# A retention layer and two feed-forward nets on one core: second products of the last token group held back into the pair loop, a copy put ahead of a cast

## The chip, the cores and the metric

The kernel runs on one core of a Trainium2 chip. The metric is the device time of one execution in microseconds (us); lower is better. TensorE (PE) multiplies, ScalarE (ACT) copies and evaluates functions, VectorE (DVE) and GpSimd (POOL) do element-wise work, SyncE (SP) starts the transfers between device memory and the core. Each engine runs its own instructions strictly in the order in which they were written; between engines, semaphores hold an instruction until its data or its buffer is there.

## The reference, cut to what matters

```python
x = retention(q, k, v)              # 4 x 768 tokens, 8 heads of 64: 3072 tokens x 512
h = x @ w_in                        # first net: 512 -> 2048
g = where(h > 0, h, exp(min(h, 0)) - 1)
x = g @ w_out                       # 2048 -> 512
h = x @ w2_in                       # second net: 512 -> 2048
g = (a0 + a1*h + a2*h**2 + a3*h**3) / (1 + |b0|*|h| + |b1|*h**2 + 1e-6)
out = g @ w2_out                    # 2048 -> 512
```

## The kernel before

**Split numbers.** Every float32 operand of a product is kept as a high part (a rounding ScalarE cast) and a low part (operand minus high part); a product is three matmuls: high by high, high by low, low by high. So each operand that is made on the chip costs one ScalarE cast and one subtract (`gh` and `gl` for a net's activations, `wo` for a slice of w_out or w2_out, `split_w`). The subtract of `wo`, of the second net's `gl` and of its tokens is GpSimd's; the subtract of the last block's `gl` is VectorE's.

**First net.** Tokens come in 6 blocks j of 512, the hidden layer in 16 slices f of 128. The loop over `(j, f)` does for each slice the first product (`g1`, 12 matmuls of 512 columns into `h`), the activation on ScalarE and VectorE, and behind `g1` the second product of the slice before (`g2`, again 12 matmuls of 512 columns, added up over f in four banks `acc`). `pend` is the slice whose second product is still to come. In the last block (`last`, j = 5) the two tiles `ha1`/`hb1` take turns as `h`, and this loop also prepares the second net: `load_c` and `split_w` bring w2_out slices, `w2_load`, `w2_sums` and `w2_units` make the combined w2_in blocks and write them to device memory, `x2_load` and `x2_step` make the first block's tokens, and `pack_load` brings the weights of the first pairs.

**Second net.** The loop over P takes a pair of slices (2p, 2p+1) at a time, 8 pairs to a token block, 48 pairs in all, and two more rounds for what is left. A pair's first product is a seven-product scheme on 2 x 2 blocks: `prod` does six matmuls of 256 columns, in the order 7, 1, 6, 4, 2, 5, 3. Partial sums are carried on by copying an accumulator into the place where the next product adds to it (`cp`, ScalarE): `s7`, `Q`, `u2` and last `R2` (in the trace: COPY s, ha, u, ha). Product 5 waits for the copy `u2`, product 3 for `R2`. Then two VectorE adds (`Xp`, `Pp`) finish the odd slice. `r_one`, `r_act` and `r_dve` evaluate the rational function of the odd slice (`b1_`) and the even one (`a1_`); `put` casts the result (`gh`), has GpSimd subtract (`gl`), and appends the 12 matmuls of the second product to the list `q2`. `take(n)` issues n matmuls from the list; a full pair has 42 matmuls of 256 columns and takes 5 + 2 + 5 + 6 + 6 = 24 of 512. The next block's tokens are made in the meantime (`x2_step` by the table `XSTEPS`: a plain name is a cast and a GpSimd subtract, a name with + is a GpSimd difference).

The first net's last two slices (f = 14, 15 of j = 5) are put into the list in pairs 0 and 1 and finished there; a pair before P = 2 has only those 12 matmuls, and its even slice's `r_one` comes a pair late:

```python
        if P < 2:
            jj, f, gh, gl = tail[P]
            g2_put(0, jj, f, gh, gl, False, f == KF - 1)
...
                take(5 - 5 * P)
...
        if P == 1:
            r_one(a1_)
            put(b1_, b1_["f"] == 1, False)
...
                take(6 if P > 1 else 0)
```

Of the kernel before, what the change touches and what calls it, by code (L numbers as in the profile page):

```python
# [9 lines left out]
F32 = mybir.dt.float32  # L10
# [75 lines left out]
def retention_ffn_kernel(ctx: ExitStack, tc: tile.TileContext, qkv, w1i, w1o, w2i, w2o, a_, b_, tab, out):  # L86
# [76 lines left out]

    def split_w(ph, f, e):
        c = W.pop((ph, f, e, "c"))
        nm = "io"[e]
        w = wp.tile([128, 2, 512], F32R, tag=f"{nm}{f}", name=f"w{nm}{f}")
# [628 lines left out]
    def fill(n):  # L796

        while nload[0] < min(nconv[0] + n, len(todo) if it > 31 else 2 * KF + 1):
            load_next()

    sums = psa.tile([128, 512], F32, tag="acc3", name="sums")
    for k in range(3):
        at_sum(4 + k, [sums[R[p], 128 * k:128 * k + 128] for p in range(2)])
    order = ["heGmg"] + ["hheGymugxw"] * 7 + ["yxhhweGmug"] + ["eGg"]
    pend = half = None
    after = False
    for it, (j, f) in enumerate(seq):
# [109 lines left out]
        if last:  # L917
            if 0 < f < KF - 1:
                load_c(f, 1)
# [4 lines left out]
            x2_step(0, ["", "B11", "+T3", "B21", "+T1", "B22 +T2", "T1", "T3 +T4", "T2", "T4", "", ""][max(f - 4, 0)])  # L924
            if f in (8, 12):
                pack_load(f // 4 - 2)
        if pend is not None:
            if f < KF - 1 or not last:
                g2(0, *pend)
            else:  # L930
                tail = [pend]
        if last:
            if 0 < f < KF - 1:
                split_w(1, f - 1, 1)
            if not f:
                load_c(f, 1)
# [20 lines left out]
    wk = ctx.enter_context(tc.tile_pool(name="wk", bufs=2, reuse_waits="tile"))  # L957
    tail.append(pend)
    q2 = []

    def take(n):
        while q2 and n >= q2[0][0]:
            k, go = q2.pop(0)
            go()
            n -= k

    def g2_put(ph, j, f, gh, gl, first, last):
        wh, wl = W[f, "o"]
        at = [slice(128 * m, 128 * m + 128) for m in range(4)]

        def one(m, a, b, start, stop):
            def go():
                if (ph, j) not in acc:
                    acc[ph, j] = [psa.tile([128, 512], F32, tag=f"acc{k}", name=f"acc{k}") for k in range(4)]
                lhsT, rhs = (a[:, at[m]], b) if ph else (b[:, at[m]], a)
                nc.tensor.matmul(out=acc[ph, j][m], lhsT=lhsT, rhs=rhs, start=start, stop=stop)  # L976
            return 1, go

        high = [[one(m, gh, wh, first, False), one(m, gh, wl, False, False)] for m in range(4)]
        low = [one(m, gl, wh, False, last) for m in range(4)]  # L980

        if last:
            for m in range(4):
                q2.extend(high[m] + [low[m]])
                if ph == 1 and j == NB - 1:
                    q2.append((0, lambda m=m: out_m(j, m)))
                elif m % 2:
                    q2.append((0, lambda m=m: out_two(ph, j, m // 2)))
        else:
            q2.extend(sum(high, []) + low)  # L990

    def out_m(j, m):
        ps = acc[1, j][m]
        ys = wk.tile([128, 512], F32, tag="su"[m % 2], name="ys", bufs=3)
        t0 = row(j, m)
        if m % 2:
            nc.scalar.mul(ys, ps, -1.0)
        else:
            nc.vector.tensor_scalar_mul(ys, ps, -1.0)
        (nc.scalar if m == 3 else nc.sync).dma_start(out=out[t0:t0 + 128, :], in_=ys)  # L1000

    def out_two(ph, j, a):
        ps = acc[ph, j]
        ys = stg.tile([128, 2, 512], F32, tag="st", name="ys")
        nc.scalar.mul(ys[:, 0], ps[2 * a], -1.0 if ph else 1.0)
        nc.vector.tensor_scalar_mul(ys[:, 1], ps[2 * a + 1], -1.0 if ph else 1.0)
        if ph == 0:
            nc.sync.dma_start(out=y1[j][:, 2 * a:2 * a + 2, :], in_=ys)
        else:
            t0 = row(j, 2 * a)  # L1010
            nc.sync.dma_start(out=out[t0:t0 + 256, :].rearrange("(a p) d -> p a d", p=128), in_=ys)

    def x2_bufs():
# [74 lines left out]
    for P in range(NB * NPR + 2):  # L1088
        more = P < NB * NPR
        j, p = divmod(P, NPR)  # L1090
        if P < 2:
            jj, f, gh, gl = tail[P]
            g2_put(0, jj, f, gh, gl, False, f == KF - 1)
        if more:
            if P < 2:
                take(5 - 5 * P)
# [55 lines left out]
        if more:  # L1152
# [81 lines left out]
```

## Time and profile before

| | |
|---|---|
| time, median of 3 runs | 1123.22 us (1123.08 to 1123.69) |
| time of the profiled execution | 1123.6 us |
| its span, first to last instruction | 1121.8 us |
| TensorE busy | 1104.0 us, 98% |
| VectorE, ScalarE, GpSimd busy | 782.6, 773.5, 420.5 us |
| granted TensorE clock | 1.00 in every window of 50 us |

What lies around the span is 1.8 us. Busy times of an engine are sums of its instructions' times; a matmul's end is modelled, so the gaps of TensorE are known to about a tenth of a microsecond. The last block of the first net runs from about 508 to 592 us, the pairs from there on.

### The profile page before, as it was taken

Reading aid. Unit: us, or ns where it says so; the run is one execution under the profiler, and the core shown is the slowest. Engines: PE = TensorE matmul, PEld = TensorE weight load, DVE = VectorE, ACT = ScalarE, POOL = GpSimd, SP = SyncE. Lnnn points to the kernel's source line nnn. Section 1 sums busy time; section 2 is a strip of 40 time slices with the busy share of each in tenths; the row PEclk is TensorE's granted clock in tenths of the full one; section 3 lists DMA queues with packets and bytes.
Section 4 is the critical chain, followed back from the end, with each engine's and each line's share of the span. In section 5 each row is a group of like instructions: output and inputs, shape, how many; then the busy total and the mean of one; then the engine's idle time right before and its main releaser. Section 6 shows DMA issues by size and latency. Waiting matters only on the chain.

```text
span 1121.8 us, 21652 instructions
## 1 busy us (share of the span) xinstructions
PE 1104.0 (98%) x8398; PEld 937.4 (84%) x8398; DVE 782.6 (70%) x1254; ACT 773.5 (69%) x1434; POOL 420.5 (37%) x322
## 2 busy tenths in 40 slices
PE   7999999999999999999998999999999999999998
PEld 6877888888888888888887888888888889888997
DVE  5997723355555454545556988888888888988986
ACT  5878734365565555445567888888888888888876
POOL 2433302344444333322451642543453452452222
PEclk9999999999999999999999999999999999999999
DMA  9576303375575435416786754855755665655641
GB/s 374 188 247 215 102 1 108 106 249 188 176 248 190 168 124 178 137 48 219 241 317 202 239 156 149 279 160 162 264 168 169 253 176 174 235 176 153 235 132 39
DMA packets 72664, 205.90 MB, mean 184 GB/s; under 512 B 8177, under 2 KB 8689, under 8 KB 72561
## 3 DMA queue, kind: packets, MB, share of 16 engines
q1 hardware_dynamic: 72272, 204.12, 54.3%
q8 instruction: 66, 1.08, 0.4%
q10 hardware_dynamic: 288, 0.40, 0.1%
q14 instruction: 38, 0.30, 0.1%
HBM read 167.79 MB, written 36.70 MB: 182 GB/s over the span
## 4 chain that ended last, share of the span: by engine, by line
PE 86%; DVE 5%; ACT 4%; issue 2%; DMA 1%; POOL 1%; SPq 0%; ACTq 0%; POOLq 0%; DVEq 0%
PE acc L976 23%; PE acc L419 20%; PE hb L1066 14%; PE r L419 12%; PE ha L1066 6%; PE h L419 4%; PE r L262 3%; PE hb L419 2%; PE ha L419 2%; DVE st L158 1%; DVE wc L160 1%; DMA ch<-in_qkv_dram 1%; DVE St L387 1%; DVE h L859 0%; ACT wc L134 0%
## 5 line engine op out<-in xcount | busy, mean ns | idle before, releaser
L1042 POOL TENSOR_TENSOR gl<-e,gh 128x512 fp32r<-128x512 f32 x96 | 129.1, 1345 | 301.9 <-ACT gh L1041 183.2
L976 PE MATMUL acc<-wo,gh 128*128 128x512 f32 x768 | 210.9, 393 | 0.0
L419 PE MATMUL acc<-gh,wo 128*128 128x512 f32 x752 | 189.8, 394 | 0.5 <-ACT ys L494 0.3
L419 PEld LDWEIGHTS acc<-gh,wo 128*128 128x128 f32 x752 | 138.9, 188 | 31.7 <-ACT ys L494 0.7
L976 PEld LDWEIGHTS acc<-wo,gh 128*128 128x128 f32 x768 | 135.3, 189 | 19.0 <-ACT gh L1041 0.3
L419 PE MATMUL r<-xh,wi 128*128 128x512 f32 x440 | 144.2, 389 | 0.0
L863 POOL TENSOR_TENSOR gl<-t,gh 128x512 fp32r<-128x512 f32 x55 | 74.9, 1362 | 174.4 <-ACT gh L861 131.5
L1056 DVE SCALAR_TENSOR_TENSOR u<-u,r 128x512 f32<-128x512 f32 x96 | 81.5, 849 | 51.9 <-ACT r L1033 51.4
L859 DVE SCALAR_TENSOR_TENSOR t<-t,r 128x512 f32<-128x512 f32 x55 | 37.7, 686 | 109.4 <-ACT t L844 106.2
L976 PE MATMUL acc<-wo,gl 128*128 128x512 f32 x384 | 106.5, 391 | 0.0
L419 PE MATMUL acc<-gl,wo 128*128 128x512 f32 x376 | 100.5, 389 | 0.0
L419 PEld LDWEIGHTS r<-xh,wi 128*128 128x128 f32 x440 | 82.6, 188 | 17.2
L1066 PEld LDWEIGHTS ha<-x,wp 128*128 128x128 f32 x576 | 76.2, 190 | 16.4 <-ACT ha L1070 15.0
L1066 PE MATMUL ha<-x,wp 128*128 128x256 f32 x576 | 87.6, 288 | 2.3 <-ACT ha L1070 2.2
L843 ACT ACTIVATE t<-r 128x512 f32<-128x512 f32 x55 | 32.8, 596 | 77.3 <-PE r L419 76.9
L419 PE MATMUL r<-xl,wi 128*128 128x512 f32 x220 | 85.6, 389 | 0.0
L976 PEld LDWEIGHTS acc<-wo,gl 128*128 128x128 f32 x384 | 72.1, 188 | 14.1 <-POOL gl L1042 0.2
L419 PEld LDWEIGHTS acc<-gl,wo 128*128 128x128 f32 x376 | 70.6, 188 | 14.7
L1066 PEld LDWEIGHTS hb<-xl,wp 128*128 128x128 f32 x576 | 75.3, 191 | 5.6 <-ACT ha L1070 1.5
L1066 PEld LDWEIGHTS hb<-xh,wp 128*128 128x128 f32 x576 | 75.4, 191 | 3.6
L1066 PE MATMUL hb<-xl,wp 128*128 128x256 f32 x576 | 76.8, 283 | 0.7 <-ACT ha L1070 0.6
L1066 PE MATMUL hb<-xh,wp 128*128 128x256 f32 x576 | 76.6, 283 | 0.0
(182 smaller groups left out, 2336.6 us busy)
## 6 DMA issues: line engine op xcount, KB each, us to landing
wp<-w2p SPq DMA_DIRECT2D x144, 512.0 KB, 4.2
ch<-in_qkv_dram SPq DMA_DIRECT2D x40, 512.0 KB, 5.4
w2p<-w2t SPq DMA_DIRECT2D x56, 256.0 KB, 2.6
wp<-w2p SPq DMA_DIRECT2D x48, 256.0 KB, 3.6
st<-in_w2i_dram SPq DMA_DIRECT2D x16, 512.0 KB, 4.4
w2s<-wc SPq DMA_DIRECT2D x32, 256.0 KB, 3.2
st<-in_w2o_dram SPq DMA_DIRECT2D x16, 512.0 KB, 4.9
st<-in_w1i_dram SPq DMA_DIRECT2D x12, 512.0 KB, 4.7
```

Source lines behind the costliest of these rows:

```text
L158: lambda: v.scalar_tensor_tensor(out=t[:, :, 0], in0=t[:, :, 1], scalar=-0x80000000, in1=t[:, :, 0], op0=ALU.bitwise_and, op1=ALU.bitwise_or),
L160: lambda: v.scalar_tensor_tensor(out=ci, in0=ci, scalar=3, in1=t[:, :, 0], op0=ALU.logical_shift_left, op1=ALU.bitwise_or),
L262: nc.tensor.matmul(out=out, lhsT=lhsT, rhs=rhs, start=start, stop=stop)
L387: nc.vector.scalar_tensor_tensor(out=S, in0=S, scalar=gc_t[:, 2 * a + z:2 * a + z + 1], in1=u[:, a, z], op0=ALU.mult, op1=ALU.add)
L419: nc.tensor.matmul(out=ps, lhsT=lh, rhs=rh, start=first and idx == 0, stop=last and idx == len(pairs) - 1)
L843: nc.scalar.activation(out=t, in_=h, func=ACTF.Relu, scale=-1.0)
L859: nc.vector.scalar_tensor_tensor(out=y, in0=t, scalar=-1.0, in1=h, op0=ALU.add, op1=ALU.max)
L863: (nc.gpsimd if y is t else nc.vector).tensor_tensor(out=gl, in0=y, in1=gh.bitcast(F32), op=ALU.subtract)
L976: nc.tensor.matmul(out=acc[ph, j][m], lhsT=lhsT, rhs=rhs, start=start, stop=stop)
L1042: nc.gpsimd.tensor_tensor(out=t["gl"], in0=t["e"], in1=t["gh"].bitcast(F32), op=ALU.subtract)
L1056: stt(out=u, in0=u, scalar=QC, in1=t["r"], op0=ALU.add, op1=ALU.mult)
L1066: nc.tensor.matmul(out=o, lhsT=ws[a], rhs=xs[b], start=start and kc == 0 and i == 0, stop=kc == 1 and i == 2, skip_group_check=True)
```

## The change

Four things are done. The list `q2`, `take` and `g2_put` are moved up, and in the first net's last block the second products go through the list as well: from slice 4 on only 9 of the 12 matmuls that a slice adds are taken behind its `g1`, so that 36 are left at the end; with slice 15 that makes 48, which pairs 0 and 1 take as any other pair takes its 24. The held-back activations get tiles of their own (`own`: former w_in tiles i7 to i12 and i13). In pairs 0 and 1 both slices' `r_one` now stand where they stand in all others. In every pair `cp(R2, Pp)` is written ahead of `put(b1_)`, and the token step `x2_step` behind it, with one cast to a pair. With the list, other work moves: the token steps of the last block begin three slices earlier, `pack_load(1)` goes from slice 12 to pair 0, `x2_load` from p = 1 to p = 0, and of the `split_w` four come in pairs 0 (two), 1 and 2, where there were two in pairs 0 and 3.

```diff
-    XSTEPS = ["", "", "B11 +T3", "B21 +T1", "B22 +T2", "T1 T3", "T2 +T4", "T4"]
+    XSTEPS = ["", "B11 +T3", "B21 +T1", "B22 +T2", "T1", "T3", "T2 +T4", "T4"]
...
+    LAG, nsp, nld = 4, [0], [0]
+    own = {f: f"i{f - 1}" for f in range(KF // 2, KF - 2)}
+    own[KF - 1] = "i13"
...
-            if f == 4:
+            if f == 1:
                 x2_load(0, *(x.rearrange("p (a t) -> p a t", a=2) for x in (ch[1][:, 1024:2048], A_b, ch[0][:, 2048:2560], ch[1][:, 2048:2560])))
...
-            if f in (8, 12):
-                pack_load(f // 4 - 2)
-        if pend is not None:
-            if f < KF - 1 or not last:
-                g2(0, *pend)
-            else:
-                tail = [pend]
+            if f == KF // 2:
+                pack_load(0)
+        if pend is not None and (not last or not f):
+            g2(0, *pend)
+        elif last:
+            g2_put(0, *pend, f == 1, False)
+            take(12 if f < LAG else 9)
         if last:
-            if 0 < f < KF - 1:
-                split_w(1, f - 1, 1)
+            while nsp[0] < min(f, (3 * f + LAG - 1) // 4):
+                split_w(1, nsp[0], 1)
+                nsp[0] += 1
...
+            while nld[0] < min(nsp[0] + 3 - (f < KF - 1), KF - 1):
+                load_c(nld[0], 1)
+                nld[0] += 1
...
+    g2_put(0, *pend, False, True)
...
-            if 0 < P and P + 1 < NB * NPR:
+            if P + 1 < NB * NPR:
                 pack_load(P + 1)
-            if p == 1 and j + 1 < NB:
+            if p == 0 and j + 1 < NB:
                 x2_load(j + 1, *x2_bufs())
...
-        if j + 1 < NB:
-            x2_step(j + 1, XSTEPS[p])
         take(5)
...
-        if P == 1:
-            r_one(a1_)
-            put(b1_, b1_["f"] == 1, False)
-        elif b1_:
+        if b1_:
             r_act(a1_, "L")
             r_act(a1_, "E")
-            put(b1_, b1_["f"] == 1, False)
             r_dve(a1_, 5)
+        elif not P:
+            split_w(1, KF - 4, 1, "i14")
+            split_w(1, KF - 3, 1, "i15")
+            load_c(KF - 1, 1)
         take(2)
         if more:
             prod(Pp, P, 5)
             cp(R2, Pp)
+        if b1_:
+            put(b1_, b1_["f"] == 1, False)
+        if j + 1 < NB:
+            x2_step(j + 1, XSTEPS[p])
+        if more:
             nc.vector.tensor_tensor(out=Xp, in0=Xp, in1=u2, op=ALU.add)
             nc.vector.tensor_tensor(out=Pp, in0=Pp, in1=s7, op=ALU.add)
...
-                if P > 1 or t is b1_:
-                    r_one(t)
-                take(6 if P > 1 else 0)
+                r_one(t)
+                take(6)
```

TensorE in pair 0, before, from products 6 and 4 (the x12) to the first products of pair 1; `acc` rows are matmuls of 512 columns from the list, and the row `ha<-xh` is a matmul that only opens pair 1's bank:

```order
L1066 MATMUL hb<-xl,wp_5833 128x256 x12
L1066 MATMUL ha<-x_5679,wp_5835 128x256 x6
L976 MATMUL acc_5493<-gl,wo_1771 128x512
L976 MATMUL acc_5494<-gl,wo_1771 128x512
L1066 MATMUL hb<-x_5680,wp_5835 128x256 x6
L1066 MATMUL ha<-x_5681,wp_5837 128x256 x6
L1100 MATMUL ha<-xh 128x512
```

The same place after the change, from product 5 (hb, x6) on; `g` is a held-back activation:

```order
L1074 MATMUL hb<-x_5773,wp_5825 128x256 x6
L819 MATMUL acc_5496<-g,wo_1630 128x512
L819 MATMUL acc_5493<-g,wo_1630 128x512
L819 MATMUL acc_5494<-g,wo_1630 128x512
L819 MATMUL acc_5495<-g,wo_1630 128x512
L819 MATMUL acc_5496<-g,wo_1630 128x512
L1074 MATMUL ha<-x_5719,wp_5827 128x256 x6
L819 MATMUL acc_5493<-g,wo_1723 128x512 x2
L819 MATMUL acc_5494<-g,wo_1723 128x512 x2
```

Before, product 3 (ha, last x6) followed on product 5 with nothing between; now five matmuls of the list stand there, and twelve more behind product 3.

ScalarE in pair 5 (p = 5), before, from the cast of the even slice of pair 3 to the first function of the new odd slice; `x` and `xh` are casts of tokens, COPY u is `u2`, COPY ha is `R2`:

```order
L1041 CAST gh<-e 128x512
L537 CAST x_6409<-xb_6269 128x512
L537 CAST xh<-xbt 128x512
L1070 COPY u_6759<-hb 128x256
L1031 ACTIVATE r<-u,lnb 128x512
L1033 ACTIVATE r<-r,lnb 128x512
L1041 CAST gh<-e 128x512
L1070 COPY ha<-hb 128x256
L1026 ACTIVATE s<-hb 128x512
```

And after:

```order
L1049 CAST gh<-e 128x512
L1078 COPY u_6754<-hb 128x256
L1039 ACTIVATE r<-u,lnb 128x512
L1041 ACTIVATE r<-r,lnb 128x512
L1078 COPY ha<-hb 128x256
L1049 CAST gh<-e 128x512
L538 CAST xh<-xbt 128x512
L1034 ACTIVATE s<-hb 128x512
```

The two token casts ahead of `u2` are gone; one stands behind `R2` and the cast of the odd slice (the other is now in pair 4).

SyncE's queue from the last slice of the first net into pair 1, after the change; `wc` is a w2_out slice, `wp` the combined weights of a pair (four transfers), `xb` the next block's tokens:

```order
L777 DMA wc<-w2s_1_128 128x512
L556 DMA wp_6134<-w2p_92 128x1024
L556 DMA wp_6136<-w2p_92 128x1024
L556 DMA wp_6138<-w2p_92 128x1024
L556 DMA wp_6140<-w2p_92 128x512
L514 DMA xb_6142<-y_1_85 128x1024
L514 DMA xb_6143<-y_1_85 128x1024
L777 DMA wc<-w2s_1_130 128x512
L556 DMA wp_6250<-w2p_93 128x1024
```

The four transfers from `w2p_92` (pair 1's weights) stood ahead of slice 13's transfers before, in the middle of the last block; now they stand behind the last `wc` load of slice 15.

## Rows read from the trace of the kernel before

**Rows 1.** The page: busy time of TensorE, share of the span, instructions.

```profile
PE 1104.0 (98%) x8398; PEld 937.4 (84%) x8398; DVE 782.6 (70%) x1254; ACT 773.5 (69%) x1434; POOL 420.5 (37%) x322
```

**Rows 2.** Windows, TensorE: stretch, length, busy (matmuls), clock, DMA share, GB/s.

```profile
500.00:550.00 50.00, 50.00 (x223) 1.00 0.65 216
...
600.00:650.00 50.00, 46.06 (x289) 1.00 0.65 216
```

**Rows 3.** Timeline, TensorE, pairs 0 to 4: start, duration, instructions, idle before.

```profile
592.57 1.60 PE L1066 MATMUL hb<-xh,wp 128*128 128x256 f32 x12
...
599.10 0.98 PE L1066 MATMUL ha<-x,wp 128*128 128x256 f32 x6 [0.45 <-ACT ha L1070]
...
608.14 0.97 PE L1066 MATMUL ha<-x,wp 128*128 128x256 f32 x6 [0.44 <-ACT ha L1070]
...
612.34 1.71 PE L1066 MATMUL hb<-xl,wp 128*128 128x256 f32 x12 [0.62 <-ACT ha L1070]
...
616.77 0.98 PE L1066 MATMUL hb<-x,wp 128*128 128x256 f32 x6 [1.54 <-ACT u L1070]
...
620.20 0.98 PE L1066 MATMUL ha<-x,wp 128*128 128x256 f32 x6 [1.29 <-ACT ha L1070]
...
623.76 1.60 PE L1066 MATMUL hb<-xh,wp 128*128 128x256 f32 x12
...
634.52 1.59 PE L1066 MATMUL hb<-xh,wp 128*128 128x256 f32 x12
```

**Rows 4.** Timeline, ScalarE: the last copy of pair 0, then copies and casts in pair 2.

```profile
598.69 0.36 ACT L1070 COPY ha<-hb 128x256 f32<-128x256 f32 x1 [1.51 <-PE hb L1066]
...
615.84 0.61 ACT L537 CAST xh<-xb 128x512 fp32r<-128x512 f32 x1
616.36 0.36 ACT L1070 COPY u<-hb 128x256 f32<-128x256 f32 x1
...
619.26 0.62 ACT L1041 CAST gh<-e 128x512 fp32r<-128x512 f32 x1 [1.16 <-DVE e L1058]
```

**Rows 5.** Windows by pair (4, 5, 9): length, then PE, PEld, DVE, ACT, POOL.

```profile
634.51:645.26 10.75, 10.75 (x67) 9.45 (x66) 9.34 (x15) 9.54 (x19) 6.81 (x5) 1.00 0.61 174
645.26:656.02 10.76, 10.57 (x65) 8.96 (x64) 8.82 (x13) 8.31 (x17) 5.49 (x4) 1.00 0.55 168
...
688.27:699.02 10.75, 10.75 (x69) 9.70 (x68) 9.17 (x15) 8.83 (x17) 2.59 (x2) 1.00 0.35 115
```

**Rows 6.** Timeline, ScalarE, pair 9: the last copy and the first function behind it.

```profile
695.05 0.37 ACT L1070 COPY ha<-hb 128x256 f32<-128x256 f32 x1
...
696.38 0.60 ACT L1026 ACTIVATE s<-hb 128x512 f32<-128x512 f32 x1 [0.97 <-DVE hb L1141]
```

**Rows 7.** Timeline: a GpSimd subtract beside VectorE, and VectorE's instruction alone.

```profile
616.01 1.28 POOL L1042 TENSOR_TENSOR gl<-e,gh 128x512 fp32r<-128x512 f32 x1 [7.33 <-ACT gh L1041]
...
616.46 1.38 DVE L1056 SCALAR_TENSOR_TENSOR u<-u,r 128x512 f32<-128x512 f32 x1
...
692.37 0.69 DVE L1056 SCALAR_TENSOR_TENSOR u<-u,r 128x512 f32<-128x512 f32 x1 [1.07 <-ACT r L1033]
```

**Rows 8.** Timeline, pairs 9 and 10: an accumulator read out, then written anew.

```profile
699.69 0.68 DVE L1006 TENSOR_SCALAR ys<-acc 128x512 f32<-128x512 f32 x1
...
700.61 1.32 PE L976 MATMUL acc<-wo,gh 128*128 128x512 f32 x5
```

**Rows 9.** Timeline, last block: two slices of TensorE, and VectorE between them.

```profile
566.73 0.39 PE L419 MATMUL hb<-xh,wi 128*128 128x512 f32 x1
...
571.26 0.43 DVE L574 TENSOR_TENSOR ha<-ch 128x256 f32<-128x256 f32 x1 [3.11 <-DMA ch<-w2s]
...
574.20 0.69 DVE L863 TENSOR_TENSOR gl<-hb,gh 128x512 fp32r<-128x512 f32 x1 [0.65 <-ACT gh L861]
...
577.61 0.39 PE L419 MATMUL hb<-xh,wi 128*128 128x512 f32 x1
```

**Rows 10.** Transfers issued from 555 to 625 us: KB each, median us to landing.

```profile
wp<-w2p SPq DMA_DIRECT2D x15, 512.0 KB, 5.1
```

More of the change, by code (lines that the diff above doesn't have):

```diff
@@ L162, in narrow_b, with split_w @@
         ]
-    def split_w(ph, f, e):
+    def split_w(ph, f, e, tag=None):
         c = W.pop((ph, f, e, "c"))
         nm = "io"[e]
-        w = wp.tile([128, 2, 512], F32R, tag=f"{nm}{f}", name=f"w{nm}{f}")
+        w = wp.tile([128, 2, 512], F32R, tag=tag or f"{nm}{f}", name=f"w{nm}{f}")
         hi, lo = w[:, 0, :], w[:, 1, :]
@@ L508, in x2_set @@
         two = [xp.tile([128, 2, 2, 512], F32R, tag=f"{nm}{n}", name=nm) for nm in ("xh", "xl")]
-        one = [wp.tile([128, 2, 512], F32R, tag=f"i{k}", name="x2") for k in ((11, 12, 13), (0, 1, 2))[n]]
-        parts = [t[:, m] for t in two for m in range(2)] + [t[:, :, :] for t in one]
-        X2[j] = {nm: p for nm, p in zip(("T3", "B11", "T2", "T4", "B21", "T1", "B22"), parts)}
+        X2[j] = {nm: p for nm, p in zip(("T3", "B11", "T2", "T4"), [t[:, m] for t in two for m in range(2)])}
     def x2_load(j, B0, B1, t3, t2):
@@ L533, in x2_split @@
             x2_set(j)
+        if nm not in X2[j]:
+            k = ("B21", "T1", "B22").index(nm)
+            X2[j][nm] = wp.tile([128, 2, 512], F32R, tag=f"i{k if j % 2 == 0 else 11 + k}", name="x2")
         t = X2[j][nm]
@@ L799, in fill, with take, g2_put, one @@
             load_next()
+    q2 = []
+    def take(n):
+        while q2 and n >= q2[0][0]:
+            k, go = q2.pop(0)
+            go()
+            n -= k
+    def g2_put(ph, j, f, gh, gl, first, last):
+        wh, wl = W[f, "o"]
+        at = [slice(128 * m, 128 * m + 128) for m in range(4)]
+        def one(m, a, b, start, stop):
+            def go():
+                if (ph, j) not in acc:
+                    acc[ph, j] = [psa.tile([128, 512], F32, tag=f"acc{k}", name=f"acc{k}") for k in range(4)]
+                lhsT, rhs = (a[:, at[m]], b) if ph else (b[:, at[m]], a)
+                nc.tensor.matmul(out=acc[ph, j][m], lhsT=lhsT, rhs=rhs, start=start, stop=stop)
+            return 1, go
+        high = [[one(m, gh, wh, first, False), one(m, gh, wl, False, False)] for m in range(4)]
+        low = [one(m, gl, wh, False, last) for m in range(4)]
+        if last:
+            for m in range(4):
+                q2.extend(high[m] + [low[m]])
+                if ph == 1 and j == NB - 1:
+                    q2.append((0, lambda m=m: out_m(j, m)))
+                elif m % 2:
+                    q2.append((0, lambda m=m: out_two(ph, j, m // 2)))
+        else:
+            q2.extend(sum(high, []) + low)
+    def out_m(j, m):
+        ps = acc[1, j][m]
+        ys = wk.tile([128, 512], F32, tag="su"[m % 2], name="ys", bufs=3)
+        t0 = row(j, m)
+        if m % 2:
+            nc.scalar.mul(ys, ps, -1.0)
+        else:
+            nc.vector.tensor_scalar_mul(ys, ps, -1.0)
+        (nc.scalar if m == 3 else nc.sync).dma_start(out=out[t0:t0 + 128, :], in_=ys)
+    def out_two(ph, j, a):
+        ps = acc[ph, j]
+        ys = stg.tile([128, 2, 512], F32, tag="st", name="ys")
+        nc.scalar.mul(ys[:, 0], ps[2 * a], -1.0 if ph else 1.0)
+        nc.vector.tensor_scalar_mul(ys[:, 1], ps[2 * a + 1], -1.0 if ph else 1.0)
+        if ph == 0:
+            nc.sync.dma_start(out=y1[j][:, 2 * a:2 * a + 2, :], in_=ys)
+        else:
+            t0 = row(j, 2 * a)
+            nc.sync.dma_start(out=out[t0:t0 + 256, :].rearrange("(a p) d -> p a d", p=128), in_=ys)
     sums = psa.tile([128, 512], F32, tag="acc3", name="sums")
@@ L849, in retention_ffn_kernel @@
         y = h if early or last else t
-        gh = gp.tile([128, 512], F32R, tag="gh", name="gh")
-        gl = gp.tile([128, 512], F32R, tag="gl", name="gl")
+        if last and f in own:
+            g = wp.tile([128, 2, 512], F32R, tag=own[f], name="g")
+            gh, gl = g[:, 0], g[:, 1]
+        else:
+            gh = gp.tile([128, 512], F32R, tag="gh", name="gh")
+            gl = gp.tile([128, 512], F32R, tag="gl", name="gl")
         low = None
@@ L957, in retention_ffn_kernel @@
     wk = ctx.enter_context(tc.tile_pool(name="wk", bufs=2, reuse_waits="tile"))
[L958 to L1011, printed above, removed]
     def x2_bufs():
@@ L1117, in retention_ffn_kernel @@
                 r_dve(b1_, k)
+        if P == 1:
+            split_w(1, KF - 2, 1, "o12")
         if a2_:
             put(a2_, False, a2_["f"] == KF - 2)
-        if j + 1 < NB:
-            x2_step(j + 1, XSTEPS[p])
         take(5)
```

23 lines of the change are left out of this document (3 added, 20 removed).

## The prediction, made before the result

> **What bounds the kernel now.** I read the page first: TensorE is busy 98% of the span [rows 1], so a change that leaves its matmuls as they are, and this one does, can only take or add gaps. Windows of TensorE over the span say where gaps are: most stretches of 50 us are full, but 600 to 650 us, the beginning of the pair loop, holds 46.06 us of work [rows 2]. The timeline of TensorE there shows the gaps one by one, and who ended them [rows 3]: 0.45 us in pair 0, 0.44 in pair 1, and 0.62, 1.54 and 1.29 in pair 2, 4.34 us in all, each in front of a product that waits for one of ScalarE's copies (`R2`, `R2`, `Q`, `u2`, `R2`). From 623.76 us on a pair follows the next after 10.76 us.
>
> The timeline of ScalarE shows why the copies are late [rows 4]: in pair 2 `u2` stands behind a token cast of 0.61 us, and `R2` behind the cast of an activation that itself waited 1.16 us for VectorE. That wait is the tail of a debt. Pair 0 has 12 list matmuls where a full pair has 24, pair 1 has 12 too, so TensorE runs through them faster than the other engines can follow, and the even slice's `r_one`, put off from pair 0 to pair 1, falls due when TensorE is already in pair 2.
>
> The windows by pair show a second, small wait [rows 5]: pair 5 has 0.19 us less TensorE work than its length, pair 4 has none. It is the pair with two token casts ahead of `u2`; pairs 13, 21, 29 and 37 show the same 0.19 or 0.20.
>
> **The boundary, step by step.** What the gaps cost is better taken from the period than from modelled ends. From pair 0's first product to pair 3's there are 31.19 us [rows 3]. Three full pairs take 3 x 10.76 = 32.28. The three of before hold 48 list matmuls instead of 72. A matmul of 512 columns costs 0.2267 us: in the last block 48 of them (24 to a slice) lie between 566.73 and 577.61 [rows 9]. So they should need 32.28 - 24 x 0.2267 = 26.84 us, and 0.23 for pair 1's opening matmul: 27.07. The excess is 4.1 us, against 4.34 summed from the rows. I take 4.2.
>
> After the change the three pairs have 72. The 36 extra ones (24 held back at the rate of three per slice from slice 4, and the 12 of slice 14) are only moved: each slice from 4 to 15 takes 9 and is shorter by 3 x 0.2267 = 0.68 us, which the pairs pay back. In place of the gap in pair 0, five matmuls stand between product 5 and product 3, 1.13 us against a wait of 0.45; pairs 1 and 2 get the same shape as any later pair, and the later ones run without a gap. So the 4.2 us should go.
>
> What is added there: two `wo` casts in pair 0 behind `u2`, one in pair 1, one in pair 2, of about the 0.61 of a token cast [rows 4]. In pair 0 ScalarE idles 1.51 us between `u2` and `R2`, until product 5 is done [rows 4]; two casts of 0.61 fit into that, and if they did not, `R2` could still be 1.13 - 0.45 = 0.68 us later than before. Pair 1 has one cast more, but no earlier pair's even slice to cast (0.62 [rows 4]). Cost between 0 (casts in the hole) and 0.6 (one cast uncovered); I take 0.2, nearer to the hole that the rows show.
>
> **The pair loop, step by step.** With one token cast to a pair, and none ahead of `u2`, the five waits of 0.19 go: 5 x 0.19 = 0.95 us. The cast moves to where ScalarE waits anyway: after `R2` it idles until both VectorE adds are done, 0.97 us in pair 9 [rows 6]. The odd slice's activation cast, now behind `R2`, goes into that same hole: 0.62 + 0.61 = 1.2 us, about as long as the hole and `R2`'s earlier start together. The activation's GpSimd subtract is later by about `R2`'s 0.37 us [rows 6]; its first matmul comes after 17 others of the list, 17 x 0.2267 = 3.9 us. Covered.
>
> What is new: in the pair p = 1 of each block the finished accumulators are read out (`ys`, two on ScalarE, two on VectorE), and now a token step falls into the same pair, at pairs 1, 9, 17, 25 and 33. GpSimd's two token instructions come behind the odd `gl` and so run while VectorE does `r_one`, whose first instruction reads two operands. How much such an instruction is held up the rows show for its like: u<-u,r took 1.38 us when it began during a GpSimd subtract, 0.69 alone [rows 7], so 0.69 more. Behind it comes the read-out of the second accumulator, done at 699.69 + 0.68 = 700.37; TensorE writes that bank two matmuls into its row, at 700.61 + 0.45 = 701.06 [rows 8]. The margin is 0.69 us. Lower bound of the cost: 0. Upper bound: a hold as long as a whole subtract, 1.28 us [rows 7], which leaves 0.59 at five places, 3.0 us. Nearest to the measured hold, the cost is about 0; I take 0.3 for all five, since hold and margin are equal.
>
> **The last block.** Its slices get shorter, 24 matmuls to 21, 5.44 to 4.76 us. The other engines must keep that pace, with two tiles between them and TensorE. The worst place of before: VectorE waited 3.11 us for a w2_in transfer and finished slice 11's `gl` at 574.20 + 0.69 = 574.89, where TensorE needs the tile again at 577.61 [rows 9]; 2.72 us to spare. Two shorter slices take 1.36 of them, and the load that is in the way (the weights of pair 0) starts by the work of an earlier slice, which takes up to 0.7 more. Some 0.7 is left; I count 0, upper bound 0.5 (the same again at the other loads). From 500 to 550 us TensorE shows no gap at all [rows 2].
>
> SyncE's queue: pair 1's weights now stand behind slice 15's last `wc` load, whose buffer comes free with slice 11's `wo` subtract. That follows slice 11's last second product, which ends where pair 0 starts, and two ScalarE casts: 2 x 0.62 + 1.28 [rows 4, 7] = 2.5 us. With 5.1 us to land [rows 10] the first of the four transfers is there at 7.6 us; pair 1 starts at 10.76 + 0.23 = 11.0. Covered by 3.4 us, and the fourth is used some 7 us later still. The next block's tokens stand behind them and are due a pair later. On GpSimd's queue the `wo` subtracts of pair 0 precede nothing that is due; in pair 1 one precedes the odd `gl`, with the 3.9 us of cover above.
>
> **Sum.** 1123.6 (the profiled execution) - 4.2 - 0.95 + 0.2 + 0.3 = 1118.95; the median of the runs shown, 1123.22, is 0.4 lower. I predict **1118.5 us**, 0.42% under the median.
>
> **A rule weighed.** VectorE's row of 1.38 beside 0.69 [rows 7] fits the Trainium skill, "SBUF — State Buffer", section "Who interferes with whom": a VectorE instruction with two SBUF inputs and a GpSimd instruction that reads SBUF exclude each other, and the later one waits until the first is through. By that rule taken to its end, two whole holds in every pair with a token step, the time would come out at about 1159 us; by the held instruction of the row it stays at 1118.5. What holds would do here, worked out from rows alone, is the first rival.
>
> **Rivals.**
> *Slower: VectorE becomes the bound of the pairs with a token step.* Mechanism: GpSimd's subtract and difference now lie under the first instruction of both `r_one`. VectorE is busy 9.34 of 10.75 us in pair 4 [rows 5], so 1.41 is free, 0.70 for each of two holds. At the measured 0.69 nothing happens; the point from which it decides is 0.70. At 0.80 each, 35 pairs (seven in five blocks) lose 2 x 0.1, 7 us: 1125.5. At the full 1.28 each pair loses 2 x 1.28 - 1.41 = 1.15, all of them 40 us. For it: hold and limit lie close. Against: pair 4 has token work and pair 9 has none, and VectorE is only 0.17 us busier there [rows 5], so that holds are rare or short. Chance 0.06.
> *The stall moves instead of going.* The `wo` casts, the pair-1 token step and the read-out press on ScalarE in pairs 0 to 2, and half of the 4.2 us stays: 1121.0 less the 0.95 either way, 1120.0 to 1121.2. For it: ScalarE is busy 9.5 of 10.75 in pair 4. Chance 0.13.
> *The last block or pair 1's weights give it back.* If the other engines could not follow 4.76 us and stayed at 5.44, TensorE would lose all of 12 x 0.68 = 8.2 us; a third of that, or weights that land 3.4 + 3 us late, gives 2.7 to 3 us back: 1121.5, no difference beyond 0.2%. Against: the spare 2.72 us at the worst place. Chance 0.08.
>
> **How the numbers follow.** A measurement here tells about 0.2% (2.2 us) from no change. The forecast's own range, with the bounds above, is 1117.5 to 1119.8, chance 0.73. Adding the case in which half the stall stays, the range is 1117.0 to 1121.0. Faster: 0.73 + 0.13 less a sliver beyond the line, 0.85. Same: 0.08. Slower: 0.07, the VectorE case and a worse form of the third.
>
> **What would show it.** TensorE's timeline from pair 0 on without gaps over 0.2 us, and a distance of 10.76 from pair to pair (pairs 0 and 1 0.23 more); slices 4 to 15 of the last block at 4.76; no gap in pairs 5, 13, 21, 29, 37. Wrong would be: gaps ended by `ys` or VectorE at pairs 2, 10, 18; `r_one`'s first VectorE instruction stretched in every token pair, with VectorE busy over 10.5 of 10.75; a gap at pair 1's first product ended by a transfer; gaps between slices 8 and 13.

## The result, and the profile after

The changed kernel takes 1110.76 us, median of 4 runs (1109.55 to 1111.66), against 1123.22 before: a ratio of 0.9888, 95% interval 0.9871 to 0.9905. That is 12.5 us less where 4.7 were forecast, and outside the range. The profiled execution took 1111.66 us with a span of 1109.7, 12.1 us less than the span before.

The page of the changed kernel, span and busy times. TensorE has less busy time than before with the same 8398 matmuls [rows 1]:

```profile
span 1109.7 us, 21633 instructions
...
PE 1094.9 (99%) x8398; PEld 940.0 (85%) x8398; DVE 786.2 (71%) x1254; ACT 782.0 (70%) x1434; POOL 420.1 (38%) x322
```

9.1 us of "busy" time have gone, though no matmul has. So part of what the rows of before called busy was waiting. The timeline of TensorE after, first product of pairs 0 to 4, answers to [rows 3]:

```profile
589.33 1.59 PE L1074 MATMUL hb<-xh,wp 128*128 128x256 f32 x12
...
600.08 1.60 PE L1074 MATMUL hb<-xh,wp 128*128 128x256 f32 x12
...
610.60 1.60 PE L1074 MATMUL hb<-xh,wp 128*128 128x256 f32 x12
...
621.11 1.59 PE L1074 MATMUL hb<-xh,wp 128*128 128x256 f32 x12
...
631.63 1.59 PE L1074 MATMUL hb<-xh,wp 128*128 128x256 f32 x12
```

The distance from pair to pair is 10.52 us (10.75 for pair 0, with pair 1's opening matmul in it), not 10.76. Read from the starts of all 48 pairs and averaged over four blocks (pairs 8 to 39), by the place p of the pair in its block:

| distance to the next pair, us | p=0 | 1 | 2 | 3 | 4 | 5 | 6 | 7 |
|---|---|---|---|---|---|---|---|---|
| before | 10.52 | 10.52 | 10.77 | 10.75 | 10.75 | 11.28 | 10.81 | 10.75 |
| after | 10.52 | 10.52 | 10.59 | 10.55 | 10.52 | 10.52 | 10.52 | 10.52 |

Before, the two pairs of a block without a token cast ran at 10.52 already. The first products of pairs 8, 9 and 10 in the trace of before show it:

```profile
678.14 1.59 PE L1066 MATMUL hb<-xh,wp 128*128 128x256 f32 x12
...
688.66 1.59 PE L1066 MATMUL hb<-xh,wp 128*128 128x256 f32 x12
...
699.18 1.59 PE L1066 MATMUL hb<-xh,wp 128*128 128x256 f32 x12
```

Each pair with one cast was 0.23 to 0.25 longer, the pair with two 0.76, the one behind it 0.29.

Where the span's 12.1 us come from, by the starts of the first products:

| stretch | before | after | difference |
|---|---|---|---|
| start to pair 0 | 592.57 | 589.33 | -3.24 |
| pair 0 to pair 3 | 31.19 | 31.78 | +0.59 |
| pair 3 to pair 47 (44 distances) | 472.62 | 463.29 | -9.33 |
| pair 47 to the end | 25.42 | 25.30 | -0.12 |

29 list matmuls (6.57 us) moved from the first stretch into the second. Without them the first is 3.33 us longer than before, and the second 5.98 shorter.

Why did the profile of before call a waiting engine busy? Rows of before, pairs 9 and 10, product 3 in each, and in pair 10 ScalarE's queue ahead of its copy `R2`:

```profile
695.73 0.87 PE L1066 MATMUL ha<-x,wp 128*128 128x256 f32 x6
...
703.29 0.61 ACT L537 CAST xh<-xb 128x512 fp32r<-128x512 f32 x1
...
705.46 0.60 ACT L1041 CAST gh<-e 128x512 fp32r<-128x512 f32 x1
...
705.97 0.36 ACT L1070 COPY ha<-hb 128x256 f32<-128x256 f32 x1
...
706.38 0.77 PEld L1066 LDWEIGHTS ha<-x,wp 128*128 128x128 f32 x6 [0.40 <-ACT ha L1070]
706.38 0.98 PE L1066 MATMUL ha<-x,wp 128*128 128x256 f32 x6
```

In pair 10 product 3 starts right behind the end of `R2` (705.97 + 0.36 = 706.33); it waited. Its matmul row shows no idle time, because the modelled end of the matmul before reaches over the wait; all that the row gives away is 0.98 for 0.87. The weight load's row has the wait, 0.40 us, and its releaser. Grouped over 656 to 1085 us, 40 pairs before, the weight loads of products 2 and 3 and of product 5 (idle time and its releaser are the last columns):

```profile
L1066 PEld LDWEIGHTS ha<-x,wp 128*128 128x128 f32 x480 | 63.6, 190 | 11.8 <-ACT ha L1070 10.6
...
L1066 PEld LDWEIGHTS hb<-x,wp 128*128 128x128 f32 x240 | 33.1, 188 | 6.1 <-ACT u L1070 3.1
```

and the same groups after (the window now holds 41 pairs):

```profile
L1074 PEld LDWEIGHTS ha<-x,wp 128*128 128x128 f32 x492 | 67.2, 190 | 3.5
...
L1074 PEld LDWEIGHTS hb<-x,wp 128*128 128x128 f32 x246 | 34.5, 188 | 3.7
```

10.6 and 3.1 us of waiting for ScalarE's copies stood in the profile of before, and I read the matmul rows alone. The Trainium skill, "Perfetto Trace Analysis", section "Identifying the Most-Contended Engine", says that matmul busy time is not a good measure of how close TensorE is to its limit, and names its share of the peak rate and the busy share of the weight loads instead. The rows here agree with the first half: the 98% of before held these waits. The busy share of the weight loads hardly moved, 84% before and 85% after; what told was their idle time, with its releaser.

### The profile page after: what moved, and what is told of

Read it like the earlier page. It is cut to its first block, busy times and chain, and to the rows that moved or that the text cites. A ratio compares the mean times of both kernels' runs of the same rounds, so it can differ in the third digit from the quotient of the medians.

```text
span 1109.7 us, 21633 instructions
## 1 busy us (share of the span) xinstructions
PE 1094.9 (99%) x8398; PEld 940.0 (85%) x8398; DVE 786.2 (71%) x1254; ACT 782.0 (70%) x1434; POOL 420.1 (38%) x322
## 4 chain that ended last, share of the span: by engine, by line
PE 87%; DVE 5%; ACT 3%; issue 2%; DMA 2%; POOL 1%; SPq 0%; ACTq 0%; DVEq 0%; POOLq 0%
PE acc L819 27%; PE acc L419 17%; PE hb L1074 15%; PE r L419 12%; PE ha L1074 6%; PE h L419 4%; PE r L262 3%; PE hb L419 1%; PE ha L419 1%; DVE st L158 1%; DMA ch<-w2s 1%; DMA ch<-y 1%; DVE wc L160 1%; DMA ch<-in_qkv_dram 1%; DVE St L387 1%
## 5 line engine op out<-in xcount | busy, mean ns | idle before, releaser
L419 PE MATMUL acc<-gh,wo 128*128 128x512 f32 x640 | 162.2, 395 | 0.5 <-ACT ys L494 0.3
L419 PEld LDWEIGHTS acc<-gh,wo 128*128 128x128 f32 x640 | 117.9, 188 | 27.4 <-ACT ys L494 0.7
L1056 DVE SCALAR_TENSOR_TENSOR u<-s,b,u 128x512 f32<-128x512 f32 x96 | 94.3, 982 | 1.3 <-ACT u L1036 1.3
L1064 DVE SCALAR_TENSOR_TENSOR u<-u,r 128x512 f32<-128x512 f32 x96 | 66.4, 691 | 40.3 <-ACT r L1041 40.3
L419 PE MATMUL acc<-gl,wo 128*128 128x512 f32 x320 | 85.5, 389 | 0.0
L1074 PE MATMUL ha<-x,wp 128*128 128x256 f32 x576 | 84.2, 282 | 0.0
L1074 PEld LDWEIGHTS ha<-x,wp 128*128 128x128 f32 x576 | 78.6, 190 | 4.1
```

The lines of the kernel that those rows point to most:

```text
L419: nc.tensor.matmul(out=ps, lhsT=lh, rhs=rh, start=first and idx == 0, stop=last and idx == len(pairs) - 1)
L1056: stt(out=u, in0=s, scalar=b1, in1=u, op0=ALU.mult, op1=ALU.add)
L1064: stt(out=u, in0=u, scalar=QC, in1=t["r"], op0=ALU.add, op1=ALU.mult)
L1074: nc.tensor.matmul(out=o, lhsT=ws[a], rhs=xs[b], start=start and kc == 0 and i == 0, stop=kc == 1 and i == 2, skip_group_check=True)
```

## The experiments

The theory after the result: a ScalarE token cast ahead of `u2` makes `u2` and `R2` late in every pair that has one, and the new order of a pair, not the held-back products, brings most of the gain. The rivals: GpSimd's token work and its holds on VectorE are what makes those pairs long; or holding back is what the pairs gain from. Each kernel was timed in 5 rounds beside the kernel before (1123.26 to 1123.31 us).

**R2 ahead of the cast, alone.** On the kernel before:

```diff
             r_one(a1_)
-            put(b1_, b1_["f"] == 1, False)
...
-            put(b1_, b1_["f"] == 1, False)
             r_dve(a1_, 5)
         take(2)
         if more:
             prod(Pp, P, 5)
             cp(R2, Pp)
+        if b1_:
+            put(b1_, b1_["f"] == 1, False)
+        if more:
```

> The kernel before with one edit: the cast of the odd slice (put of b1_) stands behind the copy R2 instead of ahead of it; the token steps stay where they are, two casts in one pair. Theory: in each pair with a token cast ahead of u2, R2 ends about 0.24 us too late for product 3, which the trace hides in modelled matmul ends; R2 ahead of a cast of 0.6 us takes more than that off, so the pairs with one cast go to 10.52 us, the pair with two keeps about 0.3 to 0.5 (it waits for u2), and the wait for R2 in pair 2 shrinks by some 1.3 us: 1114.5 to 1116.5 us. Rival (the token pairs are long for another reason, GpSimd's token work holding VectorE): pairs stay at 10.76, only pair 2 gains: 1121.5 to 1123.2.

1117.35 us (1117.06 to 1118.21), ratio 0.9951 [0.9938, 0.9963]. The pairs with one cast come to 10.54 and pairs 0 to 2 gain 1.55 us, as the theory has it. It misses its range by 0.9 us, for two reasons: p = 5 keeps 10.98, about as expected, since `u2` itself is late behind two casts, but the next pair inherits the delay and keeps 10.82; and part of the wait at the boundary moves into pair 3, which now takes 11.71 us where it took 10.76.

**Token step behind R2, alone.** On the kernel before:

```diff
-        if j + 1 < NB:
-            x2_step(j + 1, XSTEPS[p])
         take(5)
...
             cp(R2, Pp)
+        if j + 1 < NB:
+            x2_step(j + 1, XSTEPS[p])
+        if more:
```

> The kernel before with one edit: the token step stands behind the copy R2 instead of ahead of u2; the odd slice's cast stays ahead of R2, and one pair in eight keeps two token casts. Theory: without a token cast ahead of u2 and R2 all pairs run at the 10.52 us of the pairs without tokens, the pair with two casts perhaps 0.1 more; pair 2 loses its wait for u2 as well: 1110.5 to 1112.5 us. Rival (GpSimd's token work): it now lies under other VectorE instructions, but as much of it, so the time stays within 1 us of 1123.

1114.21 us (1113.6 to 1115.64), ratio 0.9925 [0.9912, 0.9939]. All 44 distances from pair 3 on are 10.52, also that of the pair with two casts: 462.88 us in all. The range is missed by 1.7 us because pairs 0 to 2 gain nothing (31.21 for 31.19). The timeline of TensorE in pair 2 of this kernel shows where that went:

```profile
615.90 0.98 PE L1066 MATMUL hb<-x,wp 128*128 128x256 f32 x6 [1.04 <-ACT u L1070]
...
619.86 0.98 PE L1066 MATMUL ha<-x,wp 128*128 128x256 f32 x6 [1.81 <-ACT ha L1070]
```

`u2` is waited for 0.50 us less than in [rows 3], `R2` 0.52 more: with the token cast out of the way, the copy still stands behind an activation cast that waits for VectorE.

**The whole order of a pair, nothing held back.** Both edits, the new table and the tokens loaded at p = 0:

```diff
-    XSTEPS = ["", "", "B11 +T3", "B21 +T1", "B22 +T2", "T1 T3", "T2 +T4", "T4"]
+    XSTEPS = ["", "B11 +T3", "B21 +T1", "B22 +T2", "T1", "T3", "T2 +T4", "T4"]
...
-            if p == 1 and j + 1 < NB:
+            if p == 0 and j + 1 < NB:
...
-        if j + 1 < NB:
-            x2_step(j + 1, XSTEPS[p])
         take(5)
...
-            put(b1_, b1_["f"] == 1, False)
...
             cp(R2, Pp)
+        if b1_:
+            put(b1_, b1_["f"] == 1, False)
+        if j + 1 < NB:
+            x2_step(j + 1, XSTEPS[p])
```

> The kernel before with the whole new order of a pair (R2 ahead of the odd slice's cast, token step behind both, one cast to a pair, tokens loaded at p = 0), and nothing held back: the last block and pairs 0 and 1 as before. Theory: the 10.2 us of pairs 3 to 47 go, and of the 4.8 us at the boundary the part that R2 and u2 behind casts cost, some 2; the last block loses nothing: 1110.5 to 1112 us, as fast as the whole change or within 1 us of it. Rival (holding back is what the pairs gain from): 1118 us or more.

1113.1 us (1112.95 to 1113.27), ratio 0.9911 [0.9897, 0.9924]: 10.2 of the 12.5 us. Pairs 3 to 47 need 463.76 us, as after the whole change (463.29) but for 0.45 in pair 3; pairs 0 to 2 gain 1.07. The range is missed by 1.1 us, because the boundary gives about 1 us of the some 2 expected.

**Only the held-back products.** The changed kernel with the old order of a pair:

```diff
-    XSTEPS = ["", "B11 +T3", "B21 +T1", "B22 +T2", "T1", "T3", "T2 +T4", "T4"]
+    XSTEPS = ["", "", "B11 +T3", "B21 +T1", "B22 +T2", "T1 T3", "T2 +T4", "T4"]
...
-            if p == 0 and j + 1 < NB:
+            if p == 1 and j + 1 < NB:
...
+        if j + 1 < NB:
+            x2_step(j + 1, XSTEPS[p])
         take(5)
...
+            put(b1_, b1_["f"] == 1, False)
             r_dve(a1_, 5)
...
-        if b1_:
-            put(b1_, b1_["f"] == 1, False)
-        if j + 1 < NB:
-            x2_step(j + 1, XSTEPS[p])
```

> The changed kernel with the old order of a pair (odd slice's cast ahead of R2, token step ahead of u2, two casts in one pair, tokens loaded at p = 1): only the held-back second products, the order of pairs 0 and 1 and the moved splits and loads are left. Theory: pairs 3 to 47 need 10.76 again, the boundary gains up to 4.8 us less what pair 2's token cast costs, and the last block gives 2.3 to 2.7 us back: 1120 to 1121.5 us. Rival (holding back is what the pairs gain from): under 1114 us.

1120.31 us (1119.33 to 1122.96), ratio 0.9976 [0.9966, 0.9985]: 2.95 us less than before. From pair 3 on the distances are those of before (472.51 for 472.62); pairs 0 to 2 take 32.06 with 29 more matmuls, so the boundary is healed but for the 0.27 us of pair 2's token cast. The two parts make 10.2 + 2.95 = 13.1 against 12.5: the 1.07 us that the order alone gains in pairs 0 to 2 belongs to the same waits that the held-back products remove, and is not there to be had twice.

**Is it the ScalarE cast or GpSimd's work?** Two kernels. In the first the cast stays ahead of `u2` and only GpSimd's instructions go behind `R2` (`x2_split` and `x2_sum` put them into the list `pool` instead of issuing them; that part is left out here):

```diff
+        pool = []
         if j + 1 < NB:
-            x2_step(j + 1, XSTEPS[p])
+            x2_step(j + 1, XSTEPS[p], pool)
         take(5)
...
             cp(R2, Pp)
+        for go in pool:
+            go()
```

> The kernel before with the token step split: its ScalarE cast stays ahead of u2 (two in one pair), its GpSimd subtract and difference are issued behind R2, where the change has them. Theory (the ScalarE cast ahead of u2 is the cost): pairs 3 to 47 keep 10.76 and 11.28, 1122.3 to 1123.6 us. Rival (GpSimd's token work is the cost and its new place the cure): pairs of 10.52 as with the whole step moved, 1113.5 to 1116 us.

1122.97 us (1122.65 to 1123.87), ratio 0.9997 [0.9988, 1.0006]; the pairs stay at 10.76 and 11.25. In the second, copies are added where there was no token step, ahead of `u2` at p = 0 and 1:

```diff
+        if P > 7 and more and p in (0, 1):
+            for n in range(2):
+                cp(spare_t, W[0, "o"][0][:, 256 * n:256 * n + 256].bitcast(F32))
```

> The kernel before with two ScalarE copies of 256 columns (about 0.6 us together, into a spare tile, of a constant tile) added ahead of u2 in the pairs p = 0 and p = 1 from pair 8 on, which have no token step: ten pairs. No GpSimd or VectorE instruction is added. Theory (a ScalarE cast ahead of u2 and R2 is the whole cost): these pairs go from 10.52 to about 10.75, in all 2.0 to 2.6 us more than before: 1125.2 to 1125.9 us. Rival (GpSimd's token work holding VectorE, or the transfers of the tokens): they stay at 10.52 and the time within 0.5 us of 1123.2.

1128.72 us (1128.3 to 1129.05), ratio 1.0048 [1.0035, 1.0061], slower as the theory wants, but by 5.5 us instead of 2.0 to 2.6. The ten pairs go to 10.97, and the pairs p = 2 behind them from 10.77 to 10.93: 10 x 0.45 + 4 x 0.16 = 5.1 us. The timeline of pair 9 of this kernel, TensorE and ScalarE:

```profile
693.26 0.84 ACT L1070 CAST spare<-wo 128x256 fp32r<-128x256 f32 x2
...
694.00 0.37 ACT L1070 COPY u<-hb 128x256 f32<-128x256 f32 x1
...
694.42 0.98 PE L1066 MATMUL hb<-x,wp 128*128 128x256 f32 x6
...
696.16 0.37 ACT L1070 COPY ha<-hb 128x256 f32<-128x256 f32 x1
...
696.58 0.98 PE L1066 MATMUL ha<-x,wp 128*128 128x256 f32 x6
```

The two copies take 0.84 us, not 0.6, and both products now start when their copy ends: one wait for `u2` and one for `R2`, 0.22 us each. Together the two kernels settle it: casts make the pairs long without any GpSimd work, and moving GpSimd's work without the casts changes nothing.

**One cast to a pair, still ahead of u2.** The table and the load at p = 0 alone:

```diff
-    XSTEPS = ["", "", "B11 +T3", "B21 +T1", "B22 +T2", "T1 T3", "T2 +T4", "T4"]
+    XSTEPS = ["", "B11 +T3", "B21 +T1", "B22 +T2", "T1", "T3", "T2 +T4", "T4"]
...
-            if p == 1 and j + 1 < NB:
+            if p == 0 and j + 1 < NB:
```

> The kernel before with the new table of token steps alone (one cast to a pair from p = 1 on, tokens loaded at p = 0), still ahead of u2. Theory: the pair of two casts falls from 11.28 to 10.76 and the one behind it from 10.83 to 10.76, while p = 1 rises from 10.52 to 10.76 or a little more because the accumulators are read out there: 5 x 0.35 = 1.7 us less, with up to 1 us either way at the boundary, where a token cast moves from pair 2 to pair 1: 1120.5 to 1122.5 us. Rival (two casts in one pair are the cost, as I had it in the prediction): all pairs at 10.52 but p = 1, 1113 to 1115 us.

1123.59 us (1123.18 to 1124.07), ratio 1.0001 [0.9992, 1.0010]. Neither my estimate nor the rival: the pair of two falls to 10.75, but p = 1 rises to 10.76 and p = 2, where the accumulators are read out, to 11.08. The waits of a block are spread otherwise and are as long; at the boundary 0.9 us come on top. One cast to a pair is worth nothing by itself.

**The last block.** What the change gave back there: the timeline after, TensorE's gaps, VectorE and GpSimd at slices 9 to 13.

```profile
558.34 1.30 POOL L539 TENSOR_TENSOR xh<-ch,xh 128x512 fp32r<-128x512 f32 x1 [1.50 <-ACT xh L538]
...
558.50 1.43 DVE L575 TENSOR_TENSOR ha<-ch 128x256 f32<-128x256 f32 x1
...
559.60 1.47 POOL L527 TENSOR_TENSOR A<-A,ch 128x512 f32<-128x512 f32 x1
...
560.31 1.05 DVE L575 TENSOR_TENSOR hb<-ch 128x256 f32<-128x256 f32 x1
...
563.82 0.50 PE L419 MATMUL hb<-xh,wi 128*128 128x512 f32 x1 [0.65 <-DVE g L925]
...
570.98 0.43 DVE L575 TENSOR_TENSOR ha<-ch 128x256 f32<-128x256 f32 x1 [2.58 <-DMA ch<-w2s]
...
574.67 0.50 PE L419 MATMUL hb<-xh,wi 128*128 128x512 f32 x1 [1.03 <-DVE g L925]
```

TensorE waits twice for VectorE's low part: once behind two sums that run long beside GpSimd's instructions (1.43 and 1.05 us for 0.43 alone), once behind a late w2_in transfer. Two variants of the changed kernel, and the kernel itself beside them:

> The changed kernel once more, so that the variants of its last block have it on the same chip: 1109.5 to 1111.7 us, two gaps of about 0.8 and 1.2 us in the last block, ended by VectorE's low part of a held-back activation.

1111.42 us (1110.99 to 1111.85), ratio 0.9894 [0.9881, 0.9908]; gaps of 0.63 and 0.61 at the same slices where 0.8 and 1.2 were expected, and one of 0.31 in slice 3, ended by ScalarE's cast `gh`. Beside the kernel before in these rounds the change is worth 11.8 us, in the result above 12.5.

```diff
-            if f == KF // 2:
+            if f == KF - 3:
                 pack_load(0)
```

> The changed kernel with the weights of pair 0 loaded at slice 13 instead of slice 8. Theory: the 1.2 us gap comes from VectorE waiting 2.6 us for a w2_in transfer that queues behind these weights; it goes, the 0.8 us one stays (VectorE held up by GpSimd): 1.0 to 1.4 us under the changed kernel beside it. Rival (VectorE cannot keep a slice of 4.76 us anyway): the gap moves to a later slice and the time stays within 0.4 us.

1113.35 us (1112.66 to 1114.56), ratio 0.9913 [0.9899, 0.9926], 1.9 us slower than the changed kernel, a miss. The second gap is gone but for 0.16 us, and VectorE's wait for the transfer with it, but the weights now stand ahead of slice 11's `wc` load. ScalarE and TensorE in pair 0 of this kernel:

```profile
593.43 0.62 ACT L169 CAST wo<-wc 128x512 fp32r<-128x512 f32 x1 [4.27 <-DMA wc<-w2s]
...
594.65 1.71 PE L1074 MATMUL hb<-xl,wp 128*128 128x256 f32 x12 [3.27 <-ACT ha L1078]
```

A `wo` cast waits 4.27 us for its transfer, and pair 0's copies queue behind it on ScalarE. The mechanism of the second gap was right; that all else would stay as it was, was not.

```diff
-            take(12 if f < LAG else 9)
+            take(12 if f < LAG or 8 <= f < 12 else 9 if f < 12 else 6)
```

> The changed kernel with the same 36 second products held back, but at other slices: three each at slices 4 to 7, none at 8 to 11, six each at 12 to 15. Theory: the slices that VectorE is late for keep 5.44 us, so both gaps go, and the slices of 4.08 us at the end have no token step and are followed: 1.5 to 2.2 us under the changed kernel. Rival (4.08 us is too short for ScalarE's and VectorE's work of a slice): gaps of more than 1 us at slices 12 to 15, no gain.

1109.31 us (1108.44 to 1109.6), ratio 0.9876 [0.9861, 0.9891]: 2.1 us under the changed kernel on the same chip, every run under every run of it, and the fastest kernel of this study. Both gaps are gone, though the two sums of slice 9 run as long as before; what is left in the block is a gap of 0.44 us at slice 4 (0.75 by the starts of the slices). VectorE's two sums, that gap, and in ScalarE's queue the token cast ahead of it:

```profile
557.68 1.43 DVE L575 TENSOR_TENSOR ha<-ch 128x256 f32<-128x256 f32 x1
...
559.48 1.06 DVE L575 TENSOR_TENSOR hb<-ch 128x256 f32<-128x256 f32 x1
...
531.42 2.12 PE L819 MATMUL acc<-gh,wo 128*128 128x512 f32 x8 [0.44 <-ACT gh L923]
...
527.72 0.62 ACT L538 CAST xh<-ch 128x512 fp32r<-128x512 f32 x1 [2.15 <-DMA ch<-y]
```

The cast waits 2.15 us for its tokens, and slice 3's activation, which ends in that `gh`, stands behind it on ScalarE. The changed kernel has the same wait (1.89 us) and loses 0.4 us there. The change has moved the token steps three slices earlier; that this is what the 0.4 us cost is read from the rows, no run moves them alone.

## Why the prediction was wrong, by its own steps

**The step that failed: "the later ones run without a gap", and with it "five waits of 0.19" for the pair loop.** I took 10.76 us as the period of a pair that waits for nothing, and the 0.19 us of the five pairs with two casts as the whole of the pair loop's waiting. Both came from TensorE's matmul rows, in windows cut at 10.75 us. The pair that waits for nothing needs 10.52, and pairs 9 and 17, without tokens, showed it. The term of 0.95 measured 9.74: so much pairs 3 to 47 gain (472.62 to 462.88 us) when only the token step's place is changed, with every pair at 10.52. In the whole change it is 9.33, the read-out below taken off. The mechanism that I gave for the pair of two casts, a token cast ahead of `u2`, holds for all token pairs; in those with one cast it is `R2` that comes late.

**The boundary, 4.2 us.** Right in place and cause, too small in size: 5.98. Two errors. The window from pair 0's first product holds 43 list matmuls, not 48, since pair 0 takes its first 5 ahead of it; and the period of 10.76 counted waits as work. With 43 and 10.52 the excess of before is 31.19 - (31.56 - 29 x 0.2267 + 0.23) = 5.97. The visible gaps of [rows 3], 4.34 us, are short by 1.6: each of the five waits is about a quarter of a microsecond longer than its row says, and a sixth, in pair 1 in front of products 6 and 4, leaves no idle time in the matmul rows (the weight load's row has 0.48 us). Pairs 0 to 2 now take 31.78, what the sum without waits gives (31.79).

**What the casts cost in pairs 0 to 2, 0.2 us.** Nothing that the distances show.

**The read-out, 0.3 us for five places.** The size came out, 0.41 us over the 10.52 of a free pair, but by luck: the wait that costs is another one. Where the prediction looked for it there is none. The hold came as foreseen, 1.42 us in place of 0.75 beside the token's GpSimd subtract; VectorE's read-out ends at 695.76 + 0.68 = 696.44, and TensorE needs the bank at 696.18 + 0.45 = 696.63. The changed kernel at pairs 9 and 10:

```profile
692.62 1.29 POOL L539 TENSOR_TENSOR xh<-xb,xh 128x512 fp32r<-128x512 f32 x1
693.04 1.42 DVE L1056 SCALAR_TENSOR_TENSOR u<-s,b,u 128x512 f32<-128x512 f32 x1
...
695.76 0.68 DVE L849 TENSOR_SCALAR ys<-acc 128x512 f32<-128x512 f32 x1
...
696.18 1.32 PE L819 MATMUL acc<-wo,gh 128*128 128x512 f32 x5
```

Of the 0.41 us, 0.27 lie in pair 34, which takes 10.79. In the whole pair loop the weight loads' rows show two waits: 0.20 us in front of pair 27's first product and 0.47 in front of pair 35's. Pair 35 in the changed kernel: VectorE's last read-out, SyncE's store of it and the first of the pair's weights behind that store, with their time to landing, then VectorE's instruction that the row names, and the wait:

```profile
950.95 0.68 DVE L849 TENSOR_SCALAR ys<-acc 128x512 f32<-128x512 f32 x1
...
951.70 0.39 SPq L854 DMA_DIRECT2D out_dram<-ys  x1
952.18 0.42 SPq L556 DMA_DIRECT2D wp<-w2p  x1
...
DMA to landing us min/median/max: 5.8/5.8/5.8
...
956.34 1.21 DVE L1056 SCALAR_TENSOR_TENSOR u<-s,b,u 128x512 f32<-128x512 f32 x1
...
958.05 1.49 PEld L1074 LDWEIGHTS hb<-xh,wp 128*128 128x128 f32 x12 [0.47 <-DVE u L1056]
```

VectorE's instruction had ended at 957.55. The weights landed at 952.18 + 5.8 = 957.98, and the weight load starts at 958.05. They were issued late because SyncE's queue held the store of the read-out ahead of them, until VectorE had done it at 951.63. Before, the first weights of pairs 11, 19, 27 and 35 were there 1.2 to 1.6 us ahead of need, after the change 0.1 to 0.8. What of this comes from the hold and what from the earlier loads of the tokens, no run separates.

**The last block, counted as 0, at most 0.5.** Wrong: 2.3 us around the two gaps and 0.4 at slice 4, by the starts of the slices; the other 0.6 of the 3.33 lies in the kernel's first 50 us, which the change does not touch and which differ by as much between other runs. The step that failed is "two shorter slices take 1.36 of them". That is right if VectorE keeps its distance from the slice it works on, and it does not. Slice 9's first matmul and its low part, before:

```profile
555.85 0.39 PE L419 MATMUL hb<-xh,wi 128*128 128x512 f32 x1
...
562.78 0.69 DVE L863 TENSOR_TENSOR gl<-hb,gh 128x512 fp32r<-128x512 f32 x1 [0.65 <-ACT gh L861]
```

and after:

```profile
553.46 0.39 PE L419 MATMUL hb<-xh,wi 128*128 128x512 f32 x1
...
563.08 0.69 DVE L925 TENSOR_TENSOR g<-hb,g 128x512 fp32r<-128x512 f32 x1 [0.65 <-ACT g L923]
```

The low part ended 7.6 us behind the slice's start before and 10.3 after: each shorter slice in which VectorE and ScalarE do not follow adds its 0.68, on top of the 1.36. The two long sums are part of it (before, one of the two was long, 1.42 us), and I had not weighed them; but the last variant has them too (1.43 and 1.06 us), with slices of 5.44 around them and no gap, so it takes the shorter slices as well. No run takes GpSimd's instructions away.

**SyncE's queue.** Right: no wait in pair 1 is ended by a transfer. How near the limit the queue is, the variant with later weights shows, and pair 35 above.

**The rivals.** VectorE did not become the bound: in pair 10, with a hold and two read-outs, it is busy 10.38 of 10.55 us, and TensorE does not wait for it there. The stall did not stay: pairs 0 to 2 need no more than 10.52 each and the opening matmuls. The last block did give something back, 2.7 us, hidden under a gain three times as large as forecast.

## What to carry to other kernels

Before a period is called free of waiting, compare it with the shortest one of the same work in the same trace; here two pairs of eight had the answer. Read a matmul engine's waits in the weight loads' rows. And put a copy that the next product waits for ahead of every cast that nothing waits for yet: here that order brought 10.2 us, the held-back work 2.95.

## What was not expected of the hardware

A wait that costs 0.24 us before a product leaves no idle time in the matmul rows, only a group of six that takes 0.98 us for 0.87; the weight load's row shows 0.40. Where a longer gap is shown, the distance lost is about 0.2 us more than the row says: 0.84 and 1.19 from slice to slice in the last block, for 0.65 and 1.03. So the gaps of TensorE are not known to a tenth of a microsecond, as I had put it ahead of the prediction.

A VectorE sum of 0.43 us, whose operands both lie in the core's memory, took 1.43 beside a GpSimd subtract, more than three times as long. Two such sums in a slice stood ahead of the low part that TensorE waited for when the slices had become shorter.
